# Second routing of a three-layer kernel: flags summed by a full matmul, next thresholds from a base, ScalarE's copies later, and new numbers in the plan that orders the engines

## The chip, the cores and the metric

One core of one Trainium2 chip. The metric is the device time of one execution in microseconds (us). In tables and rows PE is TensorE (PEld its weight loads), DVE VectorE, ACT ScalarE, POOL GpSimd, SP SyncE.

## The reference

An attention with a window and block sums gives 3072 tokens of 512 numbers; a first mixture of 8 experts follows (each token goes to its best expert); the change lies in the second mixture, which gives every expert at most 384 tokens by a greedy order:

```python
def _moe2_ref(x, w_gate, w1, w2):
    N, D = x.shape; E = w_gate.shape[1]; cap = N // E
    logits = x @ w_gate
    flat = logits.flatten(); order = np.argsort(-flat)
    assigned = -np.ones(N, dtype=np.int64); counts = np.zeros(E, dtype=np.int64)
    for idx in order:
        tok, e = (int(idx) // E, int(idx) % E)
        if assigned[tok] >= 0 or counts[e] >= cap: continue
        assigned[tok] = e; counts[e] += 1
        if (assigned >= 0).all(): break
    out = np.zeros((N, D), dtype=np.float32)
    for e in range(E):
        mask = assigned == e
        out[mask] = np.maximum(x[mask] @ w1[e], 0.0) @ w2[e]
    return out
```

## The kernel before

Three stages follow each other: attention (its last matmul with V starts at 166 us of the profile), the first mixture (`phase_b`, to about 310 us), the second mixture (`phase_d`, from 310 us to the end).

**Routing.** The greedy order is found in eight phases (`Route2.phase`, 0 to 7); each fixes one expert and its 384 tokens. A phase takes for every token the best expert still open (`v`, `p_cand`, `p_oh`: tokens lie on 128 partitions x 24 columns). It then seeks a threshold at which some expert is full, in five steps (`NSTEP`). A step lays 31 thresholds on a grid (`p_thr`, L800), compares all tokens with them (`p_g`, L805, 128x768), counts per expert with matmuls (L814 in phase 0, 24 of them; L818 after that, 12 in phases 1 and 2, 6 in phases 3 to 6, where `wide` is 4), takes the counts from what is left in each expert (`p_d`, L821, `p_sat`, L827), and makes of it 31 flags, one for each partition. The number of flags that are set gives the next, finer grid (`th`, L838). In phases 0 and 1 a matmul with ones sums the flags over the partitions (L837). In phases 2 to 6 VectorE does it alone: four copies of the flags (`p_an`, L831), a 32x32 transpose (L832) and a sum (L833). Phase 7 has no search.

After the search `gl` (L843) marks the tokens above the two last thresholds, ScalarE copies it to `p_gl` (L844), `p_og` and `p_rs` (L846, L849) count them, and matmuls sum over partitions (L855) and give positions (L870, L871). ScalarE also turns the one-hot `p_oh` round into `p_ohe` (L794). `Route2.list` makes of the positions the indices of the phase's tokens: matmul into `dx_ps` (L907 or L910), then `p_ix`.

**Expert.** GpSimd gathers the 384 rows in three indirect DMAs (`xg`, L951), TensorE transposes each block of 128 (L962), ScalarE and VectorE split the block in a high and a low part (`dxh`, `dxl`, L965). L1 is 8 groups of 12 matmuls (three for each of 4 slices: L973, L974, L975; 384 columns); after each group ScalarE writes `dhh` (L978) and VectorE `dhl` (L980). L2 is 3 blocks of 24 matmuls (L987 to L989; 512 columns), each with a copy `dz` (L992) and a scatter by GpSimd (L994). Weights are split in high (`wh`, ScalarE, L935) and low (`wl`, GpSimd, L944) parts.

**Order.** Nothing moves at run time: Python code in `phase_d` writes every engine's instructions in one order, by a planned clock. `now` is TensorE's planned time, which each `yield` of `L1` and `L2` moves by a number (0.5 for three L1 matmuls, 0.65 for three L2 matmuls). `dve` and `pool` are the planned ends of VectorE's and GpSimd's work, moved by `busy(x)`. The routing is a thread whose yields give a latency and the TensorE time of what follows; its next part is written when `now` has passed `dve` plus a margin:

```python
        busy(lat); th[1]=dve[0]+(0.4 if curp>0 else 0.1); ...
        if th[0] is not None and now[0]>=th[1]:
            now[0]+=th[3]
```

So the routing of phase p+1 is strewn into the matmuls of expert p or p-1, the gather of an expert comes after its list, and its transposes (`xts_step`) at 4.5 planned us or more behind the gather. Phase 0 and its list have no expert beside them.

## Time and profile before

| | us |
|---|---|
| median of 3 runs | 673.27 |
| lowest, highest | 668.29, 679.38 |
| profiled execution, own time | 666.27 |
| its span | 664.6 |
| TensorE busy in the span | 596.7 |
| VectorE busy | 468.8 |
| GpSimd busy | 384.9 |
| ScalarE busy | 325.0 |

The span is the part of the execution that the profile shows; 1.7 us lie around it. Matmuls overlap in the profile (each lasts longer than the distance to the next), so the distance between starts is what a matmul takes of TensorE. In rows of the time line a bracket at the end gives how long the engine stood idle before the instruction and what released it.

### The profile page before, as it was taken

To read this page: it belongs to the slowest core of one execution; us is meant where nothing else is said; L and a number is where in the kernel's file an instruction comes from. 1 tells how busy PE (TensorE), PEld (TensorE's weight loads), DVE (VectorE), ACT (ScalarE), POOL (GpSimd) and SP (SyncE) were. 2 spreads that over 40 slices of the span, in tenths; PEclk is the share of its full clock that TensorE was granted. 3 is DMA by queue.
4 is the path that set the end of the run, shared out by engine and by line. 5 is a ranking of instruction groups with operands and counts; after the bars stand their busy time and mean duration, and the time that the engine had idled before them with its cause. 6 is when DMAs were issued, how large, how long until landed. Compare 5 with 4: busy or idle time off the path is not lost.

```text
span 664.6 us, 12771 instructions
## 1 busy us (share of the span) xinstructions
PE 596.7 (90%) x4424; PEld 486.6 (73%) x4427; DVE 468.8 (71%) x1811; ACT 325.0 (49%) x704; POOL 384.9 (58%) x424
## 2 busy tenths in 40 slices
PE   7786998999889999997369999999999999999995
PEld 5664877887667777774248788787878878788894
DVE  6774898998796899674766778787878877842110
ACT  5564776888436776640034153542535344263510
POOL 5225654653154688961038196693948759398931
PEclk9788998999789999997579999999999999999998
DMA  9899999939309867700071463515546262476101
GB/s 255 259 231 249 244 286 259 281 94 337 124 16 361 285 245 250 267 20 9 1 247 57 142 207 109 176 65 185 165 143 191 86 192 88 162 253 243 41 0 47
DMA packets 48481, 114.22 MB, mean 172 GB/s; under 512 B 7041, under 2 KB 7809, under 8 KB 48416
## 3 DMA queue, kind: packets, MB, share of 16 engines
q1 hardware_dynamic: 35168, 72.84, 35.5%
...
q14 instruction: 30, 0.25, 0.1%
...
## 4 chain that ended last, share of the span: by engine, by line
PE 23%; DVE 12%; issue 7%; POOL 5%; ACT 3%; DMA 2%; POOLq 0%; DVEq 0%; ACTq 0%
PE dz_ps L987 4%; PE dz_ps L988 4%; PE dz_ps L989 4%; POOL wl L944 4%; PE dh_ps L973 3%; PE dh_ps L975 3%; PE dh_ps L974 3%; ACT wh L935 2%; DVE p_g L805 1%; DVE dhl L980 1%; DVE p_an L831 1%; DMA wraw<-in_w1b_dram 1%; DVE p_d L821 1%; ACT dhh L978 1%; PE rt_ps L818 1%
## 5 line engine op out<-in xcount | busy, mean ns | idle before, releaser
L944 POOL TENSOR_TENSOR wl<-wraw,wh 128x512 fp32r<-128x512 f32 x124 | 155.7, 1294 | 5.4 <-ACT wh L935 5.1
L973 PE MATMUL dh_ps<-dxh,wh 128*128 128x384 f32 x256 | 89.9, 351 | 0.7 <-DVE dxl L965 0.7
L975 PE MATMUL dh_ps<-dxh,wl 128*128 128x384 f32 x256 | 87.5, 342 | 1.3 <-POOL wl L944 1.3
L974 PE MATMUL dh_ps<-dxl,wh 128*128 128x384 f32 x256 | 87.3, 341 | 0.9 <-DVE dxl L965 0.9
L987 PE MATMUL dz_ps<-wh,dhh 128*128 128x512 f32 x192 | 79.6, 415 | 0.0
L989 PE MATMUL dz_ps<-wh,dhl 128*128 128x512 f32 x192 | 75.9, 395 | 0.0
L988 PE MATMUL dz_ps<-wl,dhh 128*128 128x512 f32 x192 | 75.9, 395 | 0.0
L935 ACT CAST wh<-wraw 128x512 fp32r<-128x512 f32 x128 | 74.1, 620 | 3.1 <-DMA wraw<-in_w1b_dram 2.6
L994 POOL DMA_INDIRECT out_dram<-dz,io x24 | 24.4, 1016 | 79.0 <-ACT dz L992 62.5
L980 DVE SCALAR_TENSOR_TENSOR dhl<-dh_ps,dhh 128x384 fp32r<-128x384 f32 x64 | 35.1, 554 | 49.5 <-ACT dhh L978 49.4
L120 POOL TENSOR_TENSOR wraw<-wraw 96x512 f32<-96x512 f32 (+4 forms) x39 | 39.9, 1023 | 51.0 <-DMA wraw<-in_v_dram 48.6
L978 ACT ACTIVATE dhh<-dh_ps 128x384 fp32r<-128x384 f32 x64 | 31.1, 493 | 65.0 <-PE dh_ps L975 65.0
L140 ACT ACTIVATE p_e<-s_sb,nm 128x118 f32<-128x118 f32 x192 | 59.7, 386 | 0.0
L510 POOL TENSOR_TENSOR wl<-wraw,wh 128x1024 fp32r<-128x1024 f32 (+1 forms) x18 | 38.1, 2141 | 27.7 <-ACT wh L509 27.7
L509 ACT CAST wh<-wraw 128x1024 fp32r<-128x1024 f32 (+1 forms) x56 | 49.0, 934 | 7.2 <-DMA wraw<-in_w1a_dram 5.5
L951 POOL DMA_INDIRECT xg<-xrows,p_ix x24 | 23.3, 973 | 48.8 <-DVE rrow L886 29.8
L975 PEld LDWEIGHTS dh_ps<-dxh,wl 128*128 128x128 f32 x256 | 48.7, 190 | 2.7 <-POOL wl L944 2.5
L974 PEld LDWEIGHTS dh_ps<-dxl,wh 128*128 128x128 f32 x256 | 48.7, 190 | 1.7 <-DVE dxl L965 1.4
L973 PEld LDWEIGHTS dh_ps<-dxh,wh 128*128 128x128 f32 x256 | 48.6, 190 | 1.5 <-ACT dxh L965 0.9
L510 DVE TENSOR_TENSOR wl<-wraw,wh 128x1024 fp32r<-128x1024 f32 (+1 forms) x38 | 42.7, 1160 | 6.5 <-ACT wh L509 6.5
L156 PE MATMUL o_ps<-VV,pt_sb 118*64 118x65 f32 x768 | 36.9, 238 | 10.8 <-issue 6.2
L134 DVE CUSTOM_DVE_ANT_0 s_sb<-s_ps,cst 128x118 f32<-128x118 f32 x192 | 42.0, 274 | 4.2 <-PE s_ps L130 2.8
...
## 6 DMA issues: line engine op xcount, KB each, us to landing
...
```

The source lines that it names most:

```text
L134: V.tensor_tensor_reduce(out=sb[:,j,:],in0=p[:,j,0:118],in1=mk,scale=-0.125,scalar=3e38,op0=OP.add,op1=OP.min,accum_out=nm[:,j:j+1])
L140: A.activation(pe[:,j,:],sb[:,j,:],AF.Exp,bias=nm[:,j:j+1],scale=-1.0)
L509: (hi.tensor_copy if hi else nc.scalar.copy)(h[:,c],t[:,c])
L510: (lo or nc.vector).tensor_tensor(l[:,c],t[:,c],h[:,c].bitcast(F32),op=OP.subtract)
L935: A.copy(h[:,c],t[:,c])
L944: eng.tensor_tensor(l[:,c],t[:,c],h[:,c].bitcast(F32),op=OP.subtract)
L973: T.matmul(q,wh[:,c],s['xh'][:,d,:],start=(d==0),stop=False)
L974: T.matmul(q,wh[:,c],s['xl'][:,d,:],start=False,stop=False)
L975: T.matmul(q,wl[:,c],s['xh'][:,d,:],start=False,stop=(d==3))
L987: T.matmul(q,s['hh'][:,f,c0],wh[:,c],start=(f==0),stop=False)
L988: T.matmul(q,s['hh'][:,f,c0],wl[:,c],start=False,stop=False)
L989: T.matmul(q,s['hl'][:,f,c0],wh[:,c],start=False,stop=(f==7))
```

## The change

Five things are changed, all in the second mixture.

- In phases 2 to 6 the flags are summed by the matmul with ones, as in phases 0 and 1; the four copies, the transpose and the sum go. The flags `p_any` are two fixed tiles of 128 rows, cleared once by GpSimd, and the matmul takes all 128 rows.
- A `base` of 33 numbers (next grid laid on the first column of this one) is made while TensorE counts; when the sum comes, one instruction makes the next grid of it (`p_thr`), where two stood in a row (`th`, then `p_thr`). The two last thresholds come from one instruction too.
- ScalarE's `p_ohe` is written at the second step of the search, and `p_gl` after the wait for `p_og`.
- The matmul L855 is written before the four updates of `asg` instead of behind them; `fo` and the update of `rrow` come after the position matmuls.
- The plan's numbers: 0.5 becomes 0.522 for three L1 matmuls, 0.65 becomes 0.7 for three L2 matmuls, the margin 0.4 becomes 0.25, and the latencies of the routing's parts are others.

```diff
@@ Route2.__init__ and init
+        self.anys=[cp.tile([128,1],BF,name=f"p_any{i}") for i in range(2)]
+        for a in self.anys: nc.gpsimd.memset(a,0.0)
...
-        V.tensor_scalar(self.ws,self.wsc,a,2.0,op0=OP.mult,op1=OP.mult)
+        V.tensor_scalar(self.ws,self.wsc,a,2.0,op0=OP.mult,op1=OP.mult); V.tensor_scalar(self.q['ws'],self.wsc,a,2.0,op0=OP.mult,op1=OP.mult)
@@ Route2.phase
-        oh=wk.tile([128,8,24],BF,name="p_ohe"); nc.scalar.copy(oh,oc.rearrange("p c e->p e c"))
+        oh=wk.tile([128,8,24],BF,name="p_ohe")
+        def turn(): nc.scalar.copy(oh,oc.rearrange("p c e->p e c"))
...
-                if s or not ph: V.tensor_scalar(thr,Q('jr'),ws[:,s:s+1],low,op0=OP.mult,op1=OP.add)
...
-                yield ((2.3+0.2*nw if ph>=2 else 1.4) if s else 1.1),(0.7 if ph<1 else 0.8/self.wide(ph))
+                if s==1: turn()
+                yield (1.4 if s else 1.0),(0.1+0.8/n if ph else 0.7)
...
+                if s+1<NSTEP: base=wk.tile([128,33],F32,name="p_base"); V.tensor_scalar(base,Q('jr'),ws[:,s+1:s+2],thr[:,0:1],op0=OP.mult,op1=OP.add)
...
-                if ph>=2:
-
-                    an=wk.tile([128,1],F32,name="p_an4")
-                    for q in range(4): V.tensor_scalar(an[32*q:32*q+R],e,0.0,None,op0=OP.is_ge)
-                    tr=wk.tile([128,32],F32,name="p_tr"); V.transpose(tr,an.to_broadcast([128,32]))
-                    p=wk.tile([128,1],F32,name="p_cnt"); V.tensor_reduce(p,tr[:,0:J],AX.X,OP.add)
-                else:
-                    if ph: V.tensor_scalar(anys,e[0:J],0.0,None,op0=OP.is_ge)
-                    yield (0.7 if ph else 0.35),0.05
-                    p=self.psum(); T.matmul(p[:,0:1],st['ones_b'][0:J,:],anys,start=True,stop=True)
-                V.tensor_scalar(lo,p[:,0:1],ws[:,s:s+1],low,op0=OP.mult,op1=OP.add); low=lo
-            V.tensor_scalar(hi,lo,ws[:,NSTEP-1:NSTEP],None,op0=OP.add)
+                    V.tensor_scalar(anys[0:J],e,0.0,None,op0=OP.is_ge)
+                yield (0.27+0.2*n if ph else 0.35),(0.13 if ph else 0.05)
+                p=self.psum(); T.matmul(p[:,0:1],st['ones_b'],anys,start=True,stop=True)
+                if s+1<NSTEP:
+                    thr=wk.tile([128,33],F32,name="p_thr"); V.scalar_tensor_tensor(thr,Q('ws')[:,s:s+1].to_broadcast([128,33]),p[:,0:1],base,op0=OP.mult,op1=OP.add)
+                else: V.scalar_tensor_tensor(th,Q('ws')[:,s:s+1].to_broadcast([128,2]),p[:,0:1],thr[:,0:2],op0=OP.mult,op1=OP.add)
...
-        nc.scalar.copy(gs,gl)
...
-        if ph: yield (2.5 if 2<=ph<7 else 1.3 if ph else 1.0),0
+        if ph: yield 1.1,0
+        nc.scalar.copy(gs,gl)
...
-        yield 1.0,0.05
-        p=self.psum(); T.matmul(p[:,0:16],st['ones_b'],rs.rearrange("p s e->p (s e)"),start=True,stop=True)
...
-        V.tensor_sub(self.r,self.r,p[:,8:16])
-        yield 1.0,0.1
+        yield 2.1,0.15
         o=p[:,16:18]
         T.matmul(o,st['tri_b'],t2,start=True,stop=False,skip_group_check=True)
@@ phase_d, L1 and step
-            if d<3: yield 0.5
+            if d<3: yield 0.522
...
-        busy(lat); th[1]=dve[0]+(0.4 if curp>0 else 0.1); th.append(dur) if len(th)==3 else th.__setitem__(3,dur)
+        busy(lat); th[1]=dve[0]+(0.25 if curp>0 else 0.1); th.append(dur) if len(th)==3 else th.__setitem__(3,dur)
```

What that does to the order is seen at three places. The first is VectorE in phase 3, from the flags of the fourth step to the differences of the fifth. Before:

```order
L827 ISA p_e 32x1
L831 TENSOR_SCALAR p_an_6230<-p_e 32x1 x4
L832 STREAM_TRANSPOSE p_tr<-p_an_6230 128x32
L833 TENSOR_REDUCE p_cnt<-p_tr 128x1
L838 TENSOR_SCALAR th<-p_cnt,ws,th 128x1
L800 TENSOR_SCALAR p_thr<-st_ps,ws,th 128x32
L805 TENSOR_TENSOR p_g<-st_ps,p_thr 128x768
L980 SCALAR_TENSOR_TENSOR dhl<-dh_ps,dhh 128x384 x2
L821 TENSOR_TENSOR p_d<-rrow,rt_ps 32x8
```

And now (L824 is the line of `p_d`, L826 of `p_sat`, L974 of `dhl`):

```order
L826 ISA p_e 31x1
L827 TENSOR_SCALAR p_any_4617<-p_e 31x1
L974 SCALAR_TENSOR_TENSOR dhl<-dh_ps,dhh 128x384
L831 SCALAR_TENSOR_TENSOR p_thr<-st_ps,rt_ps,p_base 128x33
L806 TENSOR_TENSOR p_g<-st_ps,p_thr 128x768
L974 SCALAR_TENSOR_TENSOR dhl<-dh_ps,dhh 128x384
L824 TENSOR_TENSOR p_d<-rrow,rt_ps 32x8
```

Eight instructions between flags and comparison (with the four copies) have become one, and a `dhl` now stands ahead of `p_thr`, where both stood behind `p_g`.

The second place is TensorE at the first two transposes of phase 4's list. Before (L818 counts, L962 transposes):

```order
L818 MATMUL rt_ps<-p_oh,p_g 128x32
L987 MATMUL dz_ps<-wh,dhh 128x512
L988 MATMUL dz_ps<-wl,dhh 128x512
L989 MATMUL dz_ps<-wh,dhl 128x512
L962 MATMUL dh_ps<-cb,xg 128x128 x4
L987 MATMUL dz_ps<-wh,dhh 128x512
L988 MATMUL dz_ps<-wl,dhh 128x512
L989 MATMUL dz_ps<-wh,dhl 128x512
L962 MATMUL dh_ps<-cb,xg 128x128 x4
```

Now (L829 sums the flags, L956 transposes):

```order
L981 MATMUL dz_ps<-wh,dhh 128x512
L982 MATMUL dz_ps<-wl,dhh 128x512
L983 MATMUL dz_ps<-wh,dhl 128x512
L829 LDWEIGHTS ones_b
L829 MATMUL rt_ps<-p_any_4616,ones_b 128x1
L956 MATMUL dh_ps<-cb,xg 128x128 x4
L981 MATMUL dz_ps<-wh,dhh 128x512
L982 MATMUL dz_ps<-wl,dhh 128x512
L983 MATMUL dz_ps<-wh,dhl 128x512
L956 MATMUL dh_ps<-cb,xg 128x128 x4
```

Between the list's matmuls (L910, now L904) and the first of these transposes there stood 24 L2 matmuls and two counts; now 18 L2 matmuls, one count and one flag matmul.

The third is ScalarE at the start of phase 6. Before (L794 is `p_ohe`, L900 the list's, L992 `dz`):

```order
L978 ACTIVATE dhh<-dh_ps 128x384 x4
L794 COPY p_ohe<-p_oh 128x192
L900 ACTIVATE l_bv<-l_bh,cc 128x24x12
L992 COPY dz<-dz_ps 128x512
L935 CAST wh<-wraw 128x512 x2
```

Now (L796 is `p_ohe`, L894 the list's, L986 `dz`):

```order
L972 ACTIVATE dhh<-dh_ps 128x384 x4
L894 ACTIVATE l_bv<-l_bh,cc 128x24x12
L972 ACTIVATE dhh<-dh_ps 128x384
L796 COPY p_ohe<-p_oh 128x192
L959 CAST dxh<-dh_ps 128x4x128 x2
L986 COPY dz<-dz_ps 128x512
```

`p_ohe` stood ahead of the list's ScalarE step, and stands behind it now.

## Rows read from the trace of the kernel before

**Rows 1.** Busy us (instructions) of PE, PEld, DVE, ACT, POOL; granted clock, DMA share, GB/s.

```profile
588.00:617.00 29.00, 29.00 (x156) 26.70 (x156) 7.87 (x20) 13.55 (x26) 25.48 (x25) 1.00 0.63 228
```

**Rows 2.** TensorE's waits from 312 us on: us in total, times, longest.

```profile
PE rt_ps L855 <- DVE p_rs L849: 6.4, 5, 2.3
...
PE rt_ps L870 <- DVE rrow L867: 3.7, 7, 1.8
...
PE dh_ps L962 <- DMA xg<-xrows,p_ix: 2.6, 3, 0.9
...
PE dh_ps L975 <- POOL wl L944: 1.3, 3, 0.4
```

**Rows 3.** Time line, phase 0: from the sum of flags to the next comparison.

```profile
319.47 0.28 DVE L838 TENSOR_SCALAR th<-rt_ps,ws,th 128x1 f32<-128x1 f32 x1 [0.25 <-PE rt_ps L837]
...
320.13 0.56 DVE L805 TENSOR_TENSOR p_g<-st_ps,p_thr 128x384 bf16<-128x384 f32 x1
```

**Rows 4.** Time line, TensorE: the flags' matmul between L1 matmuls, phase 1.

```profile
362.44 0.34 PE L974 MATMUL dh_ps<-dxl,wh 128*128 128x384 f32 x1
362.61 0.34 PE L975 MATMUL dh_ps<-dxh,wl 128*128 128x384 f32 x1
362.88 0.17 PE L837 MATMUL rt_ps<-p_any,ones_b 31*128 31x1 bf16 x1
...
363.26 0.34 PE L974 MATMUL dh_ps<-dxl,wh 128*128 128x384 f32 x1
```

**Rows 5.** Time line, TensorE: one small matmul between L2 matmuls.

```profile
576.41 0.40 PE L988 MATMUL dz_ps<-wl,dhh 128*128 128x512 f32 x1
576.64 0.40 PE L989 MATMUL dz_ps<-wh,dhl 128*128 128x512 f32 x1
576.88 0.18 PE L855 MATMUL rt_ps<-p_rs,ones_b 128*128 128x16 bf16 x1
...
577.23 0.40 PE L988 MATMUL dz_ps<-wl,dhh 128*128 128x512 f32 x1
```

**Rows 6.** Time line: a list's matmul, gathers, and transposes that use them.

```profile
339.67 0.95 POOL L951 DMA_INDIRECT xg<-xrows,p_ix  x1 [0.30 <-issue]
...
343.54 0.33 PE L962 MATMUL dh_ps<-cb,xg 128*128 128x128 f32 x1 [0.94 <-DMA xg<-xrows,p_ix]
...
575.84 0.34 PE L910 MATMUL dx_ps<-l_bv,l_A 128*128 128x96 bf16 x4
...
578.13 1.01 POOL L951 DMA_INDIRECT xg<-xrows,p_ix  x1 [2.19 <-DVE st_ps L856]
...
580.71 0.95 POOL L951 DMA_INDIRECT xg<-xrows,p_ix  x1 [0.30 <-PE dz_ps L989]
...
582.30 0.27 PE L962 MATMUL dh_ps<-cb,xg 128*128 128x128 f32 x1
...
585.61 0.44 PE L962 MATMUL dh_ps<-cb,xg 128*128 128x128 f32 x2 [0.89 <-DMA xg<-xrows,p_ix]
```

**Rows 7.** Time line, ScalarE and VectorE ahead of a wait for L849.

```profile
481.31 0.20 ACT L844 COPY p_gl<-st_ps 128x48 f32<-128x48 f32 x1 [3.48 <-DVE st_ps L843]
...
482.31 1.14 ACT L935 CAST wh<-wraw 128x512 fp32r<-128x512 f32 x2
...
483.87 0.56 DVE L980 SCALAR_TENSOR_TENSOR dhl<-dh_ps,dhh 128x384 fp32r<-128x384 f32 x1 [0.86 <-ACT dhh L978]
484.35 0.54 DVE L849 TENSOR_REDUCE p_rs<-p_og 128x16 bf16<-128x384 bf16 x1
```

**Rows 8.** Time line: last matmul of an L1 group, its `dhl`; and a step's differences and flags.

```profile
360.52 0.34 PE L975 MATMUL dh_ps<-dxh,wl 128*128 128x384 f32 x1
...
361.42 0.56 DVE L980 SCALAR_TENSOR_TENSOR dhl<-dh_ps,dhh 128x384 fp32r<-128x384 f32 x1 [0.31 <-ACT dhh L978]
...
424.96 0.17 DVE L821 TENSOR_TENSOR p_d<-rrow,rt_ps 32x8 f32<-32x8 f32 x1 [0.94 <-PE rt_ps L818]
...
425.74 0.14 DVE L831 TENSOR_SCALAR p_an<-p_e 32x1 f32<-32x1 f32 x1
```

More of the change, by code (lines that the diff above doesn't have):

```diff
@@ L308, in load_const @@
     wg=cp.tile([128,32],F32,name="wg2"); nc.sync.dma_start(wg,I['wg2']); st['wg2']=wg
-    cc=cp.tile([128,38],F32,name="cc"); nc.sync.dma_start(cc,I['cc']); st['cc']=cc
+    cc=cp.tile([128,6],F32,name="cc"); nc.sync.dma_start(cc,I['cc']); st['cc']=cc
 def make_const(nc,cp,st):
@@ L739, in layout_c @@
 def layout_c(inp):
-    jr=np.tile(np.arange(1,33,dtype=np.float32),(128,1))
     ws=np.tile(np.array([2.0/32**(s+1) for s in range(5)],np.float32),(128,1))
     p0=np.arange(128,dtype=np.float32)[:,None]
-    return dict(cc=np.ascontiguousarray(np.concatenate([jr,ws,p0],1)),w1b=np.ascontiguousarray(inp['moe2_w1']),w2b=np.ascontiguousarray(inp['moe2_w2']))
+    return dict(cc=np.ascontiguousarray(np.concatenate([ws,p0],1)),w1b=np.ascontiguousarray(inp['moe2_w1']),w2b=np.ascontiguousarray(inp['moe2_w2']))
 class Route2:
@@ L793, in phase @@
         oc=wk.tile(B3,BF,name="p_oh"); V.tensor_tensor(oc,cand,mx[:,:,None].to_broadcast(B3),op=OP.is_equal)
-        oh=wk.tile([128,8,24],BF,name="p_ohe"); nc.scalar.copy(oh,oc.rearrange("p c e->p e c"))
+        oh=wk.tile([128,8,24],BF,name="p_ohe")
+        def turn(): nc.scalar.copy(oh,oc.rearrange("p c e->p e c"))
         th=self.th; lo=th[:,0:1]; hi=th[:,1:2]; ws=self.ws
         if ph<7:
-            low=self.nM
+            n=self.wide(ph) if ph else 1; thr=self.thr0
+            if ph==0: V.tensor_scalar(thr,Q('jr'),ws[:,0:1],self.nM,op0=OP.mult,op1=OP.add)
+            yield 1.2,0
             for s in range(NSTEP):
-                thr=wk.tile([128,32],F32,name="p_thr") if s else self.thr0
-                if s or not ph: V.tensor_scalar(thr,Q('jr'),ws[:,s:s+1],low,op0=OP.mult,op1=OP.add)
-                if s==0: yield 1.1,0
                 g=wk.tile([128,24,32],BF,name="p_g")
@@ L804, in phase @@
                     B=[128,c1-c0,32]
-                    V.tensor_tensor(g[:,c0:c1],v[:,c0:c1,None].to_broadcast(B),thr[:,None,:].to_broadcast(B),op=OP.is_ge)
+                    V.tensor_tensor(g[:,c0:c1],v[:,c0:c1,None].to_broadcast(B),thr[:,None,1:33].to_broadcast(B),op=OP.is_ge)
                 if s==0: next(inq,None)
-                nw=self.wide(ph) if ph>=1 else 1
-                yield ((2.3+0.2*nw if ph>=2 else 1.4) if s else 1.1),(0.7 if ph<1 else 0.8/self.wide(ph))
-                p=self.psum()
-                anys=wk.tile([J,1],BF,name="p_any")
-                if ph<1:
-                    if ph==0: T.matmul(p[0:J,0:8],st['mone'][:,0:J],st['capr'],start=True,stop=False)
-                    for c in range(24): T.matmul(p[0:J+(ph>0),0:8],g[:,c,0:J+(ph>0)],oc[:,c,:],start=(ph>0 and c==0),stop=(c==23))
+                if s==1: turn()
+                yield (1.4 if s else 1.0),(0.1+0.8/n if ph else 0.7)
+                p=self.psum(); anys=self.anys[s%2]
+                if ph==0:
+                    T.matmul(p[0:J,0:8],st['mone'][:,0:J],st['capr'],start=True,stop=False)
+                    for c in range(24): T.matmul(p[0:J,0:8],g[:,c,0:J],oc[:,c,:],start=False,stop=(c==23))
                 else:
-                    n=self.wide(ph)
                     for c in range(0,24,n): T.matmul(p[0:32*n,0:8*n],g[:,c:c+n,:].rearrange("p c j->p (c j)"),oc[:,c:c+n,:].rearrange("p c e->p (c e)"),start=(c==0),stop=(c==24-n))
+                if s+1<NSTEP: base=wk.tile([128,33],F32,name="p_base"); V.tensor_scalar(base,Q('jr'),ws[:,s+1:s+2],thr[:,0:1],op0=OP.mult,op1=OP.add)
+                if ph==0:
+                    sat=wk.tile([J,8],BF,name="p_sat")
+                    V.tensor_scalar(sat,p[0:J,0:8],0.0,0.0,op0=OP.is_ge,op1=OP.max,accum_out=anys[0:J])
+                else:
                     d=wk.tile([128,8],F32,name="p_d"); x=self.r
@@ L963, in xT @@
         c=slice(128*b,128*b+128); h=S[p]['xh'][:,:,c]
-        busy(0.65)
+        busy(0.72)
         A.copy(h,q); V.tensor_tensor(S[p]['xl'][:,:,c],q,h.bitcast(F32),op=OP.subtract)
@@ L975, in L1 @@
             T.matmul(q,wl[:,c],s['xh'][:,d,:],start=False,stop=(d==3))
-            if d<3: yield 0.5
+            if d<3: yield 0.522
         h=s['hh'][:,f,:]
         A.activation(h,q,AF.Relu)
-        busy(0.5)
+        busy(0.6)
         V.scalar_tensor_tensor(s['hl'][:,f,:],q,0.0,h.bitcast(F32),op0=OP.max,op1=OP.subtract)
-        yield 0.5
+        yield 0.522
     def L2(p,b):
@@ L1062, in phase_d @@
     while True:
-        if route[0] is None and route[2]<7 and (route[2] in routed if route[2] else 0 in listed): R.update(); busy(1.4); start_route(route[2]+1)
+        if route[0] is None and route[2]<7 and (route[2] in routed if route[2] else 0 in listed): R.update(); busy(1.25); start_route(route[2]+1)
         if (curp>=0 or xts.get(0,3)==3 or now[0]<gath_t[0]+HOLD) and try_thread(): continue
```

26 lines of the change are left out of this document (13 added, 13 removed).

## The prediction

> **What bounds the kernel now.** I read the busy time by stage first. Once routing is over, between 588 and 617 us, TensorE is busy for 29.00 of 29.00 us at a granted clock of 1.00 (2.4 GHz), with VectorE at 7.87 and GpSimd at 25.48 [rows 1]. From the first expert on, TensorE sets the pace, and routing costs time where its matmuls take TensorE's time or keep TensorE waiting. So the list of TensorE's waits comes next. From 312 us on it waits 6.4 us at L855 (five times, the longest, 2.3, in phase 0, where nothing runs beside), 3.7 at L870 (seven times, 1.8 of it in phase 0), 2.6 for gathered rows and 1.3 for `wl` [rows 2]. Beside experts that leaves 4.1 + 1.9 + 1.3 us that a better order could win, and 0.9 for gathers [rows 6]. VectorE, which the change relieves most, is no bound: a shorter chain on it pays only where TensorE now waits for it, and in phase 0.
>
> **Phase 0.** Its chain lies bare. From the sum of flags, `th` starts at 319.47 and the comparison at 320.13, 0.66 us for two instructions, the first of 0.28 [rows 3]. One instruction at half that distance, 0.33, takes their place, in four steps, and the end of the search loses one as well: 5 x 0.33 = **-1.65 us**. The `base` lies between a comparison and its count, where VectorE waits for TensorE; were it not hidden, 4 x 0.33 would be lost again. The second `ws` and L870's freedom from `rrow` are one small instruction each way and cancel.
>
> **The waits that go.** Ahead of L855 I follow one case. ScalarE reaches the copy `p_gl` early and stands 3.48 us idle at it; casts and `dhh` pile up behind, so a `dhl` starts only at 483.87 after 0.86 us of waiting, and `p_rs` behind it at 484.35 [rows 7]. The copy is now written later, when `gl` is done, and L855 stands 15 L1 matmuls behind the last flags. `p_rs` takes 0.54 [rows 7], and th, `gl` and `p_og` ahead of it, with no more elements than `p_rs` reads, no longer each: at most 4 x 0.54 = 2.2 us, and 15 x 0.17 + 0.3 = 2.9 are there; a `dhl` of 0.56 between them about fits. So **-4.1 us**; if a wait stays, 0. L870 loses its wait for `rrow` and stands 15 matmuls behind L855 in place of 9: **-1.9**. `wl` is needed at the start of an expert's L1. Around phase 4's list 48 L2 matmuls now stand between the first transpose and that L1, where 15 stood: 33 x 0.23 = 7.6 us more for GpSimd, **-1.3**.
>
> **The flags' matmul, 25 new ones (5 phases x 5 steps).** Among L1 matmuls: from L975 at 362.61 to L974 at 363.26 are 0.65 us with the flags' matmul in it, where two matmuls take 2 x 0.17 (362.44 to 362.61): 0.30 us [rows 4]. Among L2 matmuls no such one is in the trace; the nearest is a matmul with the same weights and 16 columns, 576.64 to 577.23, 0.59 against 2 x 0.23: 0.13 us [rows 5]. In the new order 9 of the 25 stand among L1, 16 among L2 or transposes: 9 x 0.30 + 16 x 0.13 = **+4.8 us**; ends 25 x 0.13 = 3.3 and 25 x 0.30 = 7.5. The matmul takes 128 rows of flags in place of 31, which L855 has too.
> The Trainium skill, in "TensorE: Matmul & The Clock Gate" (Back-to-back issue gap; LDWEIGHTS), gives a matmul of up to 64 columns an issue floor of some 25 ns, and a load of 128 columns 128/1.2 = 107 ns. An estimate from that page is 0.13 us wherever the matmul stands, 3.3 us in all, 1.5 less than I take; the rows among L1 speak against it.
>
> **Transposes that come too early.** This is the largest cost. In the trace a list's matmul starts at 575.84, the first gather at 578.13 (2.3 us later: VectorE makes the indices), and the first transpose, 6.46 us after the list's matmul, just runs [rows 6]. A gather takes 3.87 us from its start to a transpose that waited for it (339.67 to 343.54), at most 4.17 (578.13 to 582.30, no wait), once 4.90 (580.71 to 585.61) [rows 6]. So the rows are there 2.3 + 3.9 = 6.2 us after the list's matmul. In the new order there are between list and first transpose, for phase 4, 18 L2 matmuls, one count (six small matmuls, which I put at two of the one in [rows 5], 0.26) and one flags' matmul: 0.34 + 18 x 0.23 + 0.26 + 0.13 = 4.9 us. TensorE waits 1.3 us there. The other transposes stand 1.1 to 1.4 us behind, where gathers come every 1.3 (578.13 to 580.71 are two); only in phases 2 and 3 the second and third stand side by side, which adds 0.8. By the same count, with 18 to 21 L2 matmuls ahead of each first transpose (phase 6: 15 and 6 of L1): phase 1 0.4, 2 and 3 1.3 each, 4 and 5 1.4 each, 6 1.3; together 7.1, less the 0.9 that was waited: **+6.2 us**. At 3.4 us for a gather it is some 3, at 4.9 some 12.
>
> **Flags behind a `dhl`.** A step used to wait for VectorE once, at the count; now twice. A `dhl` written right behind its L1 group can't start before ScalarE's `dhh` is done: 0.90 us after the group's last matmul starts (360.52 to 361.42), and lasts 0.56 [rows 8]. The count starts 0.2 after that matmul, so `p_d` behind such a `dhl` starts 1.3 us into it; flags take 0.78 from `p_d` (424.96 to 425.74) and 0.14 + 0.1 [rows 8], 2.3 us in all, and TensorE is there after 0.26 + 9 x 0.17 + 0.1 = 1.9. That is 0.4 us at three places (phases 2, 3, 4), and by the same reckoning 0.2 at two counts behind a `p_thr` that stands behind a `dhl`, and 0.2 in phase 6: **+1.8 us**. With a cast (0.6) ahead of `dhh` each time it is 5. Where a `dhl` is an older one, nothing is waited.
>
> **Rest at nothing.** `p_ohe` is needed only at `p_og`, over a step later. The clearing of the flags' tiles lies on an idle GpSimd. Five fewer VectorE instructions a step, 0.14 to 0.28 each [rows 3, 8], free some 25 x 1 us on an engine that isn't the bound.
>
> **Sum.** -1.65 - 4.1 - 1.9 - 1.3 + 4.8 + 6.2 + 1.8 = **+3.85 us** on the profiled execution of 666.27, 670.1. The median of the runs shown is 673.27, 7.0 above that execution; the same step from there gives **677 us**, 0.6% more than before.
>
> **Rivals.**
> A, the gathers land in time. If a gather takes 3.5 us or the list's indices come sooner, and no `dhl` is in the way, the transposes cost 1 us and the flags 3.3: -8.95 + 4.3 = -4.65, 668.6 us. For it: the waiting gather of 3.87 was in a stage of little traffic, but none shorter waited in these rows. Against: in the trace the order gives a list 6.46 us and leaves nothing over.
> B, the waits are moved, not gone. `p_gl` reads a PSUM tile that VectorE works on as well; VectorE's update L848 has to wait for the copy, which may stand behind ScalarE's casts of 1.14 us [rows 7]. Then the position matmul is late by 1.14 less the 0.55 that its 15 matmuls leave over, six times: +3.5 on the forecast, 680.5 us. The Trainium skill, in "PSUM — Partial Sum Buffer" (PSUM bank collisions raise a hardware error), says that two engines may not be in one bank and quadrant at once, reads included; the diff's order leaves that wait to L848, and no row here shows its length.
> C, slower: gathers take 4.9 us as the one in phase 6 did, since the weights' loads run beside them. Six lists wait 12 us in place of 6.2, with casts ahead of `dhh` 3 more: 3.85 + 9 = +12.8, 686 us. It decides from 5.0 us on: then TensorE loses over 2%.
> D, the change doesn't shorten what paces: that holds beside experts in any case; were the routing chain itself the pace there, the 25 us above would be won, 648 us. Against it: TensorE's waits in [rows 2] are too short for that.
>
> **How the numbers follow.** Forecast (+1 to +7 us: 674 to 680) 0.50, A 0.22, B 0.14, C 0.10, D 0.01, the rest unknown. The range takes A's with the lowest run seen (668.29, 5 below the median) and C's: 665 to 687. A measurement of this kernel tells about 2% from no change, 13.5 us. Faster by more: D and an A with a low run, 0.04; slower by more: half of C and a B with C's gathers, 0.08; within 2% 0.88.
>
> **What would show it.** In the changed profile: waits at L846 and L862 (the old L855, L870) near zero; 35 flags' matmuls, VectorE's busy time down by 20 us or more; waits at L956 for gathered rows in five or six lists, 0.4 to 1.3 us each; waits at L829 of some 0.4. Wrong would make it: gathers landing within 3 us (A), long waits at L862 for L848's chain (B), an L956 that waits 3 us (C), or a routing whose lists come so late that an expert's start waits.

## The result, and the profile after

| | before | after |
|---|---|---|
| median of 20 runs each, us | 671.72 | 675.50 |
| lowest, highest | 667.68, 679.38 | 669.14, 684.84 |
| profiled execution, own time | 666.27 | 672.59 |
| TensorE busy | 596.7 | 601.6 |
| VectorE busy | 468.8 | 445.5 |

The ratio is 1.0054, with a 95% interval of 1.0027 to 1.0080: 3.6 us more (1.8 to 5.4). The two profiled executions lie 6.3 us apart, so their times alone don't measure it. VectorE has 23 us less to do (in a step of phases 2 to 6 its eight instructions between `p_e` and `p_g` have become two, `p_any` and `p_thr`, with `base` beside them), TensorE 4.9 more, and where no routing runs the picture is that of [rows 1]: TensorE 29.00 of 29.00 us.

TensorE's waits from 312 us on, in the changed kernel (us in total, times, longest):

```profile
PE dh_ps L956 <- DMA xg<-xrows,p_ix: 6.3, 7, 1.5
PE rt_ps L829 <- DVE p_any L827: 3.7, 4, 2.7
...
PE rt_ps L846 <- DVE p_rs L843: 3.3, 2, 1.8
PE rt_ps L815 <- DVE p_g L806: 2.2, 6, 0.6
...
PE rt_ps L862 <- DVE p_ei L858: 1.4, 1, 1.4
```

Against [rows 2]: the waits for p_rs have shrunk from 6.4 to 3.3 (1.8 of it is phase 0, 1.5 phase 7, which has no search), those for rrow and wl are gone (1.4 for p_ei is phase 0). In their place stand 6.3 for gathered rows (4.8 beside experts; 0.9 before), waits for the flags (3.7, of which 2.7 in expert 0) and for a comparison (2.2; 0.3 before).

The clearest view is a sum over stretches, since attention and the first mixture, which the change doesn't touch, end at 310 to 320 us, a few us apart from one execution to the next. The table takes the starts of rows in the time lines: from the reduction L734 (end of the first mixture) to expert 0's first L1 matmul, from there to expert 1's, and so on, up to the end of the last L2 matmul (its start and 0.24). Each line is one profiled execution; two of them (before, again, 676.2 us, and flags with 31 rows, 688.0) ran slower than most executions of their kernels.

| us | L734 to expert 0 | expert 0 | experts 1 to 5 | 6 and 7 | ratio, 95% interval |
|---|---|---|---|---|---|
| before | 33.4 | 45.9 | 197.7 | 68.2 | 1 |
| before, again | 34.8 | 45.9 | 198.4 | 68.2 | |
| after | 30.9 | 49.1 | 203.9 | 68.9 | 1.0054 (1.0027 to 1.0080) |
| after, again | 31.0 | 46.5 | 203.7 | 68.9 | 1.0070 (1.0034 to 1.0106) |
| transposes later | 31.8 | 48.4 | 197.6 | 68.9 | 1.0011 (0.9975 to 1.0047) |
| casts behind dhh | 31.0 | 48.3 | 203.7 | 68.9 | 1.0067 (1.0033 to 1.0101) |
| copies only | 32.6 | 47.9 | 192.6 | 68.3 | 0.9891 (0.9843 to 0.9939) |
| old plan | 31.7 | 46.6 | 218.4 | 71.4 | 1.0351 (1.0300 to 1.0402) |
| copies and base | 31.8 | 46.2 | 191.5 | 68.9 | 0.9919 (0.9880 to 0.9957) |
| same, idle flags' matmuls | 31.9 | 48.1 | 191.7 | 69.6 | 0.9919 (0.9883 to 0.9954) |
| later, flags on VectorE | 31.0 | 53.4 | 197.4 | 68.9 | 1.0018 (0.9979 to 1.0056) |
| flags with 31 rows | 31.6 | 51.2 | 207.9 | 68.9 | 1.0124 (1.0085 to 1.0163) |
| copies, base, order of sums | 31.4 | 46.7 | 194.3 | 68.9 | 0.9878 (0.9819 to 0.9937) |
| copies and base, same place | 31.3 | 49.2 | 191.6 | 68.3 | 0.9874 (0.9810 to 0.9937) |

Experts 1 to 5 repeat within 0.7 us for one order, so they tell orders apart where the times can't; expert 0 doesn't repeat (46.5 and 49.1 for the same kernel). From before to after: 2.4 to 3.9 us won in the first column, 0.6 to 3.2 lost in expert 0, 5.3 to 6.1 in experts 1 to 5, 0.6 in 6 and 7. Not all of this is the change's own. In the first column the first matmul of phase 0 starts 0.7 us after L734 in some executions and 1.4 to 1.5 in others, with either order; both profiles of before have the long one and both of after the short one, and before, again has a gather that landed late. With the same start the change wins 1.6 us there (33.4 before, 31.8 in the run with transposes later). And one count of phase 2, 12 matmuls and 0.7 us, has moved from expert 0 to expert 1.

Four places of the changed kernel's time line show where. Phase 0, VectorE, from the sum of flags to the next comparison; it answers to [rows 3], and 0.66 us from start to start have become 0.29:

```profile
317.74 0.26 DVE L831 SCALAR_TENSOR_TENSOR p_thr<-st_ps,rt_ps,p_base 128x33 f32<-128x33 f32 x1 [0.26 <-PE rt_ps L829]
318.03 1.09 DVE L806 TENSOR_TENSOR p_g<-st_ps,p_thr 128x384 bf16<-128x384 f32 x3
```

The flags' matmul among L1 matmuls (for [rows 4]) and among L2 matmuls. From L969 at 402.50 to L968 at 402.97 are 0.47 us for two L1 matmuls of 0.175, so the flags cost 0.12; from L983 at 460.12 to L982 at 460.72 0.60 for two of 0.23, so 0.14:

```profile
402.50 0.33 PE L969 MATMUL dh_ps<-dxh,wl 128*128 128x384 f32 x1
402.67 0.18 PE L829 MATMUL rt_ps<-p_any,ones_b 128*128 128x1 bf16 x1
402.71 0.42 PE L967 MATMUL dh_ps<-dxh,wh 128*128 128x384 f32 x1
402.97 0.34 PE L968 MATMUL dh_ps<-dxl,wh 128*128 128x384 f32 x1
...
460.12 0.40 PE L983 MATMUL dz_ps<-wh,dhl 128*128 128x512 f32 x1
460.36 0.18 PE L829 MATMUL rt_ps<-p_any,ones_b 128*128 128x1 bf16 x1
460.40 0.48 PE L981 MATMUL dz_ps<-wh,dhh 128*128 128x512 f32 x1
460.72 0.40 PE L982 MATMUL dz_ps<-wl,dhh 128*128 128x512 f32 x1
```

A list's matmul, its gathers and the first transpose, phase 6 (for [rows 6]). The gather starts 4.3 us after the list's matmul here (VectorE makes the first masks of phase 7 ahead of the indices), the rows are used 4.0 after that, and TensorE has stood 1.52 us at the transpose:

```profile
570.58 0.43 PE L904 MATMUL dx_ps<-l_bv,l_A 128*128 128x96 bf16 x6
...
574.91 1.00 POOL L945 DMA_INDIRECT xg<-xrows,p_ix  x1 [5.92 <-DVE p_ix L911]
...
578.95 0.66 PE L956 MATMUL dh_ps<-cb,xg 128*128 128x128 f32 x4 [1.52 <-DMA xg<-xrows,p_ix]
```

And expert 0, which the prediction left out. ScalarE stands 3.41 us at the casts of the second half of w1, whose load lands at 344.5; the first `dhh` comes behind them, `dhl` behind that, `p_d` and the flags behind `dhl`, and TensorE stops for 2.69 us:

```profile
344.50 2.18 ACT L929 CAST wh<-wraw 128x512 fp32r<-128x512 f32 x4 [3.41 <-DMA wraw<-in_w1b_dram]
...
346.59 0.48 ACT L972 ACTIVATE dhh<-dh_ps 128x384 fp32r<-128x384 f32 x1
347.10 0.56 DVE L974 SCALAR_TENSOR_TENSOR dhl<-dh_ps,dhh 128x384 fp32r<-128x384 f32 x1 [4.42 <-ACT dhh L972]
347.91 0.15 DVE L824 TENSOR_TENSOR p_d<-rrow,rt_ps 32x8 f32<-32x8 f32 x1
...
348.49 0.18 PE L829 MATMUL rt_ps<-p_any,ones_b 128*128 128x1 bf16 x1 [2.69 <-DVE p_any L827]
```

Then TensorE is granted the lower clock. By windows (columns as in rows 1), 0.50 is 1.2 GHz, and TensorE was busy for 0.26 and 1.06 of 2 us ahead of it:

```profile
345.55:347.55 2.00, 0.26 (x2) 0.00 (x0) 0.45 (x1) 1.94 (x5) 2.00 (x2) 1.00 1.02 381
347.55:349.55 2.00, 1.06 (x7) 1.06 (x8) 1.59 (x8) 0.62 (x1) 2.00 (x3) 1.00 0.39 145
349.55:351.55 2.00, 2.00 (x18) 1.54 (x16) 1.19 (x3) 1.52 (x3) 2.00 (x3) 0.54 0.03 12
351.55:353.55 2.00, 2.00 (x6) 1.70 (x6) 0.46 (x4) 0.00 (x0) 2.00 (x2) 0.50 0.00 0
```

### The profile page after: what moved, and what is told of

It is laid out like the page before. It is cut to its first block, busy times and chain, and to the rows that moved or that the text cites. A ratio compares the mean times of both kernels' runs of the same rounds, so it can differ in the third digit from the quotient of the medians.

```text
span 670.8 us, 12694 instructions
## 1 busy us (share of the span) xinstructions
PE 601.6 (90%) x4452; PEld 488.1 (73%) x4452; DVE 445.5 (66%) x1680; ACT 326.4 (49%) x704; POOL 387.5 (58%) x428
## 4 chain that ended last, share of the span: by engine, by line
PE 20%; issue 11%; POOL 11%; DVE 5%; DMA 3%; ACT 2%; POOLq 0%; DVEq 0%; ACTq 0%
POOL wl L938 9%; PE dh_ps L967 3%; PE dh_ps L968 3%; PE dh_ps L969 3%; PE dz_ps L981 3%; PE dz_ps L982 3%; PE dz_ps L983 3%; DMA xg<-xrows,p_ix 2%; ACT wh L929 1%; PE dh_ps L956 1%; DMA wraw<-in_w1b_dram 1%; POOL out_dram L988 1%; DVE p_g L806 1%; PE rt_ps L813 0%; PE rt_ps L815 0%
## 5 line engine op out<-in xcount | busy, mean ns | idle before, releaser
L968 PE MATMUL dh_ps<-dxl,wh 128*128 128x384 f32 x256 | 87.8, 343 | 1.2 <-DVE dxl L959 1.2
L969 PE MATMUL dh_ps<-dxh,wl 128*128 128x384 f32 x256 | 87.5, 342 | 0.0
L974 DVE SCALAR_TENSOR_TENSOR dhl<-dh_ps,dhh 128x384 fp32r<-128x384 f32 x64 | 35.6, 556 | 67.4 <-ACT dhh L972 66.7
L983 PE MATMUL dz_ps<-wh,dhl 128*128 128x512 f32 x192 | 76.0, 396 | 0.0
L982 PE MATMUL dz_ps<-wl,dhh 128*128 128x512 f32 x192 | 75.9, 395 | 0.0
L929 ACT CAST wh<-wraw 128x512 fp32r<-128x512 f32 x128 | 72.4, 619 | 7.1 <-DMA wraw<-in_w1b_dram 6.1
L972 ACT ACTIVATE dhh<-dh_ps 128x384 fp32r<-128x384 f32 x64 | 31.4, 491 | 74.7 <-PE dh_ps L969 66.1
L968 PEld LDWEIGHTS dh_ps<-dxl,wh 128*128 128x128 f32 x256 | 49.0, 191 | 2.0 <-DVE dxl L959 1.7
L986 ACT COPY dz<-dz_ps 128x512 f32<-128x512 f32 x24 | 14.1, 586 | 71.7 <-PE dz_ps L983 34.1
L969 PEld LDWEIGHTS dh_ps<-dxh,wl 128*128 128x128 f32 x256 | 48.9, 191 | 0.0
```

The source lines that it names most:

```text
L929: A.copy(h[:,c],t[:,c])
L968: T.matmul(q,wh[:,c],s['xl'][:,d,:],start=False,stop=False)
L969: T.matmul(q,wl[:,c],s['xh'][:,d,:],start=False,stop=(d==3))
L982: T.matmul(q,s['hh'][:,f,c0],wl[:,c],start=False,stop=False)
L983: T.matmul(q,s['hl'][:,f,c0],wh[:,c],start=False,stop=(f==7))
```

## The experiments

**Transposes later.** In the changed kernel, experts 1 to 7:

```diff
-        if ... now[0]>=gath_t[q]+4.5+1.0*xts[q] ...
+        if ... now[0]>=gath_t[q]+(6.2 if q else 4.5)+1.0*xts[q] ...
```

> The changed kernel with one number altered: the transposes of experts 1 to 7 are written 6.2 planned us behind their gather in place of 4.5. Theory (transposes stand too early): in the profile of the changed kernel TensorE waits 6.3 us for gathered rows, some 4.85 of them beside experts; with five to nine more L2 matmuls between list and transposes these go to under 1 us, a gain of about 4 us, from 1.005 to about 0.999 of the kernel before. Rival (the rows are late for a reason of their own, and whatever is written behind them waits): the wait stays or goes to the L1 that needs the transposed rows, and the ratio stays at 1.005.

The waits for gathered rows fell from 6.3 to 1.8 us, none of it beside experts, and experts 1 to 5 from 203.9 to 197.6. Part of these 6.3 us has only moved into expert 0: the count of phase 2 (0.7) and the wait ahead of expert 1's L1 shown below. Experts 0 to 5 together take 246.0 us, where the second profile of the changed kernel has 250.2: 4.2 less, as the theory says. The ratio, 1.001, agrees, but its interval (0.9975 to 1.0047) overlaps the changed kernel's. One expert shows that later isn't free. In phase 1 the transposes now stand right ahead of expert 1's L1, which waits 2.22 us for the high part of the rows and then runs for 3.4 us at 1.2 GHz, 0.32 us a matmul:

```profile
397.30 0.66 PE L956 MATMUL dh_ps<-cb,xg 128*128 128x128 f32 x4
400.18 0.44 PE L967 MATMUL dh_ps<-dxh,wh 128*128 128x384 f32 x1 [2.22 <-ACT dxh L959]
400.90 0.69 PE L968 MATMUL dh_ps<-dxl,wh 128*128 128x384 f32 x1 [0.28 <-DVE dxl L959]
401.39 0.52 PE L969 MATMUL dh_ps<-dxh,wl 128*128 128x384 f32 x1
401.71 0.52 PE L967 MATMUL dh_ps<-dxh,wh 128*128 128x384 f32 x1
```

**Casts behind dhh.** In the changed kernel:

```diff
-        if q==0: return g+4.3+2.9*j if j else f+4.3
+        if q==0: return g+8.0+2.9*j if j else f+4.3
...
-            if npc==32 and conved[curp]<12 or ...
+            if npc==16 and conved[curp]<8 or npc==32 and conved[curp]<12 or ...
...
-            if xts.get(q,0)==3 and conved.get(q,0)>=8:
+            if xts.get(q,0)==3 and conved.get(q,0)>=(8 if q else 4):
```

> The changed kernel, but expert 0 may start when the first chunk of its w1 is split, and the second chunk's casts are planned 8.0 + 2.9 us behind the gather (they were planned at 4.3 + 2.9; the chunk lands 10.9 us behind it). Theory: the four casts that wait 3.4 us for the load no longer stand ahead of ScalarE's first dhh, so the flags' matmul at 348.49 loses its wait of 2.69 us, and TensorE, which doesn't stop, keeps its 2.4 GHz between 349 and 356, where it now starts L1 matmuls 0.32 us apart in place of 0.175 (some 3 us lost): together a gain of 4 to 6 us, a ratio of 0.996 to 1.000. Rival 1 (the clock falls there whatever is waited for): only the 2.7 us, 1.001. Rival 2 (the second chunk's low half is late and the fifth L1 group waits for it): no gain, 1.005.

Nothing was won: 1.0067, expert 0 takes 48.3 us. The flags' wait is gone. But TensorE's clock fell all the same, 1.0 us into L1 and for 3.4 us, with no wait for flags near it, and at the end of expert 0 eight of expert 1's transposes now stand side by side ahead of a count of phase 2, which waits 1.84 us for its comparison:

```profile
390.37 1.42 PE L956 MATMUL dh_ps<-cb,xg 128*128 128x128 f32 x8
393.63 0.55 PE L815 MATMUL rt_ps<-p_oh,p_g 128*64 128x16 bf16 x12 [1.84 <-DVE p_g L806]
```

Rival 1 is right that the clock falls anyway, but neither rival says the rest: the loss moved to another wait of the same expert.

**Copies only.** The kernel before, with

```diff
-        oh=...; nc.scalar.copy(oh,oc.rearrange("p c e->p e c"))
+        def turn(): nc.scalar.copy(oh,oc.rearrange("p c e->p e c"))
...
+                if s==1: turn()
...
-        nc.scalar.copy(gs,gl)
...
         if ph: yield (2.5 if 2<=ph<7 else 1.3 if ph else 1.0),0
+        nc.scalar.copy(gs,gl)
```

> The kernel before with ScalarE's two copies placed as in the change (p_ohe at the second step, p_gl behind the wait for p_og) and nothing else. Theory (the copies are what delayed p_rs): the 4.1 us of waits at the matmul on p_rs beside experts go, 667.6 us where before takes 671.7, a ratio of 0.994; a trace shows that wait at under 1 us beside phase 0's 2.3. Rival (p_rs was late because its chain on VectorE is long, and the copies only lay beside it): the waits stay, ratio 1.000.

Better than the theory by time, 0.9891, or 7.3 us. The profile shows 5 us less of waits for p_rs and rrow beside experts 1 to 5, and 4.0 to 6.0 us less from L734 to the end (341.3 against 345.3 and 347.3); where the rest of the 7.3 lies is open. TensorE's order is that of before, and of the waits for p_rs (L858 here) only phase 0's is left; each wait for rrow beside experts 1 to 5 has halved as well (0.34 to 0.17). The run moves both copies, and both stood waiting in the kernel before (ScalarE idle for 37 us in all ahead of `p_ohe`, 32 ahead of `p_gl`); what each is worth alone it doesn't tell. Its waits from 312 us on:

```profile
PE rt_ps L873 <- DVE rrow L870: 2.8, 7, 1.8
...
PE rt_ps L858 <- DVE p_rs L852: 2.1, 1, 2.1
```

**Old plan.** The changed kernel with 0.5, 0.65 and 0.4 for 0.522, 0.7 and 0.25.

> The changed kernel with the plan's old numbers for TensorE and the margin (0.5, 0.65, 0.4 in place of 0.522, 0.7, 0.25); all else stays. In this order 21 L2 matmuls, two counts and a flags' matmul stand between a list and its first transposes (18 to 21, one and one in the changed kernel), but two transposes stand side by side five times. Theory (what costs is how the transposes stand, not the numbers as such): the waits for gathers stay at 4 to 5 us, the flags' waits shrink by 1 us: ratio 1.003 to 1.005. Rival (the new time model itself is the loss): ratio 0.998 or below.

Both theories fail, and in the other direction than the rival said: 1.035, 23 us slower than before. With the old numbers the same planned time covers more matmuls, and the latencies of the routing's parts, which stay new here, were set for the others. The lists of phases 2 to 6 stand behind 48 to 51 of an expert's 72 L2 matmuls, in the changed kernel behind 24, 15, 6, none and none; so the transposes end up against the next L1, and that costs twice, in waits and in clock:

```profile
477.38 0.66 PE L956 MATMUL dh_ps<-cb,xg 128*128 128x128 f32 x4 [1.49 <-DMA xg<-xrows,p_ix]
...
478.09 1.12 PE L956 MATMUL dh_ps<-cb,xg 128*128 128x128 f32 x4
479.88 0.69 PE L967 MATMUL dh_ps<-dxh,wh 128*128 128x384 f32 x1 [0.67 <-ACT dxh L959]
481.92 0.69 PE L968 MATMUL dh_ps<-dxl,wh 128*128 128x384 f32 x1 [1.35 <-DVE dxl L959]
482.40 0.52 PE L969 MATMUL dh_ps<-dxh,wl 128*128 128x384 f32 x1
```

Experts 2 to 5 in its windows (the last three numbers are clock, DMA share, GB/s), at 0.93 to 0.99 where the changed kernel has 1.00:

```profile
436.46:479.88 43.42, 39.80 (x224) 32.27 (x224) 25.91 (x98) 18.55 (x37) 28.16 (x29) 0.98 0.41 138
479.88:523.93 44.05, 40.27 (x224) 33.46 (x225) 28.45 (x102) 14.54 (x30) 27.90 (x28) 0.94 0.37 127
523.93:567.40 43.47, 39.30 (x224) 32.04 (x224) 25.88 (x98) 18.47 (x37) 28.04 (x29) 0.99 0.41 140
567.40:612.73 45.33, 40.60 (x214) 33.34 (x214) 27.98 (x109) 16.78 (x34) 28.68 (x29) 0.93 0.39 132
```

**Copies and base.** The changed kernel with the flags of phases 2 to 6 on VectorE, the plan's old numbers and latencies, and the sums where they were:

```diff
-                    V.tensor_scalar(anys[0:J],e,0.0,None,op0=OP.is_ge)
+                if ph>=2:
+                    an=wk.tile([128,1],F32,name="p_an4")
+                    for q in range(4): V.tensor_scalar(an[32*q:32*q+32],e,0.0,None,op0=OP.is_ge)
+                    tr=wk.tile([128,32],F32,name="p_tr"); V.transpose(tr,an.to_broadcast([128,32]))
+                    p=wk.tile([128,1],F32,name="p_cnt"); V.tensor_reduce(p,tr[:,0:J],AX.X,OP.add)
```

> The kernel with only ScalarE's copies moved, and to it the base and the one-instruction threshold of the change, the flags summed on VectorE as before; TensorE's order is that of the kernel before to the row. Theory (the base pays in phase 0, where nothing runs beside, and nowhere else): phase 0 shorter by 1.65 to 2.5 us, some 661 us, a ratio of 0.985 to 0.987. Rival (a shorter chain pays beside experts as well, since flags and lists come sooner): more than 4 us below the run with the copies alone, 0.983 or less; a second rival, no gain because expert 0's weights land no sooner: 0.989.

0.9919, not to be told from the copies alone by time, and outside the theory's range. The trace shows what the base pays: a step of phase 0's search takes 2.18 us (the flags' matmuls start at 322.91 and 325.09) where before takes 2.54, and experts 1 to 5 gain 1.0 us at most. So the theory's place is right, and the gain too small to be seen in the times.

**Idle flags' matmuls.** To the last kernel, ahead of the counts of phases 2 to 6:

```diff
+                    if ph>=2: T.matmul(p[:,300:301],st['ones_b'],anys,start=True,stop=True)
```

> As the run with copies and base, and 25 idle flags' matmuls beside it: in phases 2 to 6 a matmul of the ones with a flags' tile that nobody reads stands ahead of each step's counts (it adds work that the result doesn't need). Nothing waits for them and no order changes, so they show the price of the matmul alone. Theory (a fixed 0.13 us each): 3.3 us more than without, a ratio higher by 0.005. Rival 1 (0.30 us, as the row in phase 1 before): 7.5 us, higher by 0.011. Rival 2 (beside the counts they are nearly free, 0.04 us): 1 us, higher by 0.0015.

The second rival is right. Among L1 and L2 matmuls alike the counts of phases 3 to 6 with an idle matmul take 0.28 us, without it 0.25: 0.03 each, and experts 1 to 5 agree as a sum (191.7 against 191.5; single ones differ by up to 1.5, where a gather or a wait for `wl` fell otherwise). So of the 0.13 us that a lone flags' matmul costs, some 0.10 is the break in the row of L1 or L2 matmuls. One of the idle matmuls and its counts:

```profile
511.44 0.18 PE L815 MATMUL rt_ps<-p_any,ones_b 128*128 128x1 bf16 x1
511.47 0.30 PE L816 MATMUL rt_ps<-p_oh,p_g 128*128 128x32 bf16 x6
```

**Flags on VectorE in the new order.** Transposes later as in the first run, and the flags' diff of the run with copies and base.

> The changed kernel with the transposes written later (as in the first run) and with the flags of phases 2 to 6 summed on VectorE as before (its latencies in the plan as before). Theory (what is left of the loss is the flags' matmuls, 3.3 us, and the waits for flags and for counts behind a dhl, 3): some 5 us below the run with late transposes alone, a ratio of 0.992 to 0.995. Rival (the shorter chain is what lets the lists come in time, so VectorE's flags bring other waits): 1.000 or above.

By time the rival: 1.0018, and experts 1 to 5 at 197.4 against 197.6. The 25 matmuls and, beside experts 1 to 5, the waits for flags are gone; waits for p_rs have grown, 5.7 us in six against 4.5 in four. But the clock differs: expert 1 runs for 10.2 us at 1.2 GHz here, and for 3.4 in the run with late transposes, and takes 43.3 us against 41.7; experts 2 to 5, at a clock of 1.00 in both, take 154.1 against 155.9. So where the clock is the same the flags on VectorE win 1.8 us, and what the clock took in expert 1 (and in expert 0, 53.4 us at a clock of 0.87) hides it. Whether that loss belongs to the order is open; the medians, 672.85 and 673.20, show no gain. The 6.1 us of experts 1 to 5 that lie between transposes later and copies and base (197.6, 191.5) are then, as an estimate from the rows, 23 flags' matmuls of 0.13 (3.0), the lower clock in expert 1 (1.7) and 1.8 more of waits, 0.4 too much in sum.

**The changed kernel again.** No edit.

> The changed kernel once more, for a second profile of the same order. Theory (the wait of 2.69 us for expert 0's first flags is not the change's: the load's landing against the start of L1 differs from one execution to the next): this profile shows another wait there, between 0 and 2.7 us, while the waits for gathered rows beside experts stay at 4 to 5 us; the ratio lies between 1.003 and 1.008. Rival (that wait belongs to the order): 2.5 us or more again.

The theory's numbers: 1.40 us in place of 2.69, and experts 1 to 5 repeat to 0.3 us each. Its reason is not borne out: the other runs that move the copies wait there too, 0.55 to 2.85 us, but for the one with the casts behind. What sets the length is said at the second profile of the kernel before, below.

**Flags with 31 rows.** In the changed kernel:

```diff
-                p=self.psum(); T.matmul(p[:,0:1],st['ones_b'],anys,start=True,stop=True)
+                p=self.psum(); T.matmul(p[:,0:1],st['ones_b'][0:J],anys[0:J],start=True,stop=True)
```

> The changed kernel, but the flags' matmul takes 31 rows of ones and flags in place of 128, as the one of the kernel before did in phase 1. TensorE's order is that of the changed kernel. The row in phase 1 of the kernel before showed 0.30 us among L1 matmuls; the changed kernel shows 0.13 at most of its flags' matmuls, among L1 and L2 alike. Theory (the 31 rows are what made it 0.30): some 0.17 us more at each of 30 flags' matmuls beside experts, 5 us, a ratio higher than the changed kernel's by 0.007 (1.012 to 1.015); the trace shows 0.30 in place of 0.13. Rival (a load's time goes by its columns, not by its rows; the 0.30 was a short wait for the flags): 0.13 as before, the ratio unchanged at 1.005 to 1.007.

The theory: 1.0124, and each flags' matmul that stands alone costs 0.30 us where it cost 0.13. Experts 1 to 5 take 4.1 us more than in the changed kernel, but that this is near 23 x 0.17 = 3.9, for the 23 that lie in them, is partly luck: expert 1 ran for 3.4 us at 1.2 GHz in this profile, which by itself makes it some 1.7 longer (half of 3.4), and the waits came out 0.8 shorter. The same place as in phase 2 above, a flags' matmul between L1 matmuls; from L969 at 415.65 to L968 at 416.31 are 0.66 us, so 0.31:

```profile
415.65 0.34 PE L969 MATMUL dh_ps<-dxh,wl 128*128 128x384 f32 x1
415.92 0.09 PEld L829 LDWEIGHTS <-ones_b 31*128 31x128 bf16 x1 [0.25 <-issue]
415.92 0.17 PE L829 MATMUL rt_ps<-p_any,ones_b 31*128 31x1 bf16 x1
416.02 0.44 PE L967 MATMUL dh_ps<-dxh,wh 128*128 128x384 f32 x1
416.31 0.34 PE L968 MATMUL dh_ps<-dxl,wh 128*128 128x384 f32 x1
```

**Copies, base and the order of the sums.** The run with copies and base, with L846 ahead of the updates and `fo` and `rrow` behind the position matmuls.

> The run with copies and base, and to it the order of the change on VectorE around the sums: the matmul on p_rs ahead of the four updates, fo and the update of rrow behind the position matmuls. TensorE's order is still that of the kernel before. Theory (the wait for rrow ahead of the position matmuls is the update's, and goes with it): 0.16 us of wait and 0.15 of delay less at each of six position matmuls, 1.5 to 2 us, some 0.002 below the run with copies and base; the trace shows no wait for rrow. Rival (the updates now stand between p_rs and p_ei, so the position matmul waits for p_ei): waits of the same size there, no gain.

The rival, and more than it said: the wait for rrow is gone, and one of 0.54 to 0.57 for p_ei stands in its place (0.17 for rrow in the run without), in expert 5 two, of 0.91 and 0.46. Experts 1 to 5 take 2.8 us more, and these waits are 2.7 of it. The ratios of the two runs, 0.9878 and 0.9919, can't show it. In the changed kernel the position matmul doesn't wait beside experts because its latency in the plan, 2.1, puts it 15 matmuls behind L846 and not 9.

**The kernel before again.** No edit.

> The kernel before once more, for a second profile. Theory (expert 0's first wait and TensorE's clock in it differ from one execution to the next, the rest is set by the order): a wait of 0 to 2.7 us for the first flags, and the same waits as in the first profile from expert 1 on: 4 of about 1 us for p_rs, six of 0.16 to 0.35 for rrow; from the end of the first mixture to the last L2 matmul 343 to 348 us, where the first profile has 345.3 and the changed kernel has 352.7 and 350.0. Rival (the order alone sets it): 345.3 within 0.5.

The theory for all but expert 0: from expert 1 on the waits repeat to 0.1 us but for one gather that landed 0.7 later, and the stretch is 347.3 us. Expert 0 has no wait for flags again, and 45.84 us after 45.93. That doesn't show the old order free of it. In both profiles of before the lower clock begins 0.8 to 0.9 us into L1, so TensorE reaches the first flags only 6.2 us after L1's start, and they are just ready then (6.1 and 6.3). In the other runs they are ready after 6.3 to 7.7 us. Where the lower clock comes ahead of them there, TensorE arrives after 6.1 to 6.9 us and waits 0 to 1.5; where it comes only later, TensorE arrives after 4.6 to 4.7 and waits 2.3 to 2.9. So how long it waits goes with where the clock falls, and the flags come up to 1.5 us later in the new orders; what the order before would wait at 2.4 GHz no run shows.

**Same place.** To the run with copies and base:

```diff
+        pad=wk.tile([128,224],F32,name="pad"); nc.gpsimd.memset(pad[0:1,0:1],0.0)
```

> The run with copies and base again, with an unused tile of 896 bytes a partition ahead of the second mixture's work tiles. In every kernel made from the changed source, experts 6 and 7, beside which no routing runs, take 35.04 and 33.82 us, in the kernel before and in the one with the copies alone 34.80 and 33.45; L1 matmuls of expert 7 start 176.6 ns apart against 173.5, at a granted clock of 1.00 in both. The new constants moved dxh, dxl, dhh and dhl by 128 bytes; the unused tile moves them to where they lay before, up to a multiple of 1024. Theory (the place of these tiles sets the pace): 34.80 and 33.45 again, some 0.25 to 0.35 us less in each of eight experts, 2 to 3 us in all, a ratio lower by 0.003 to 0.005 than the 0.992 of the run without the tile. Rival (the pace has another cause): 35.04 and 33.82.

Experts 6 and 7 take 34.81 and 33.44 us again: the theory. Beside routing little comes of it (191.6 after 191.5, 0.4 more of gathers' waits in it), so 1 us in all and not 2 to 3. The unused tile moves all work tiles behind it, so which of them counts is not told. Within the intervals the ratio of 0.9874 is that of the run without the tile. This kernel, the copies alone and the run with copies and base all beat both kernels, the one before by about 1%.

## Why the prediction was right, and where its terms were not

The time (677 forecast, 675.5 measured; +3.85 us forecast, +3.6 by the runs) and the course of it were right: waits at p_rs and rrow go, transposes written too early and flags behind a `dhl` bring as much and more. Several terms were mis-sized, others were left out, and that they cancel to 0.3 us is luck.

- **Phase 0, -1.65.** Measured -1.6 at expert 0's first L1 matmul. From the first flags' matmul to the one on p_rs 10.8 us in place of 12.6 (the shorter wait for p_rs is in it); the first step is 0.3 longer, ahead of the position matmul 0.3 is won. Right, and the two small terms cancel as said.
- **The waits that go, -4.1, -1.9, -1.3.** The copies alone take the 4.1 at p_rs away, as forecast; in the changed kernel 1.5 came back in phase 7, whose p_rs now stands behind phase 6's indices on VectorE. The waits at L870 (now L862) and at `wl` are gone beside experts.
- **The flags' matmul, +4.8.** Mis-sized: 0.12 to 0.14 us nearly everywhere, 25 x 0.13 = 3.3, the lower end. The five of phase 1 fell from 0.30 to 0.13 with the change as well, up to 5 x 0.17 = 0.85 us that the prediction didn't count (two show it; the others stand at a wait or at the lower clock). The step that failed is the price among L1 matmuls: the 0.30 of [rows 4] belongs to a matmul of 31 rows, and the prediction, which saw that the new one takes 128 rows like L855, gave it the price of the 31 rows among L1 matmuls all the same. The estimate of 3.3 us from the Trainium skill, "TensorE: Matmul & The Clock Gate" (Back-to-back issue gap; LDWEIGHTS), was the better one.
- **Transposes too early, +6.2.** Right in kind, too large in size: waits of 4.8 us beside experts in both profiles against 0.9, +4.0, and the 60 transposes of experts 1 to 5 take 1.2 us more themselves (6.6 from start to start, waits left out, in place of 5.4). List by list it is less right: 0, 1.3, 0.4, 0.9, 0.7 and 1.5 us for phases 1 to 6, where 0.4, 1.3, 1.3, 1.4, 1.4 and 1.3 were forecast. In phases 4 and 5 the gathers took 3.3 to 3.5 us and not 3.9; in phase 6 the size agrees by luck, since its gather starts 4.3 us behind the list's matmul and not 2.3. The run with later transposes took the waits beside experts away.
- **Flags behind a dhl, +1.8.** Too small: from expert 1 on 1.0 us at the flags and 2.2 at comparisons, +3.2. The prediction counted the flags' waits and took two of the others at 0.2; there are six, 0.15 to 0.6.
- **Left out.** Expert 0 (+0.6 to +3.2): ScalarE's casts of the load's second half begin 3.4 to 3.5 us into its L1, where they began 1.4 and 2.5 us into it before, and the first flags are ready 7.3 to 7.4 us into it in place of 6.1 to 6.3; why, beyond the load's landing, no run tells. And 0.6 us in experts 6 and 7 from the place of the work tiles.
- **The plan's numbers** were priced only through the places at which instructions stand. That was enough for the forecast, but not for knowing what they are worth: with the old ones beside the new latencies 20 us are lost, with the old latencies too, and the flags on VectorE (copies and base), none.

Rival A, with gathers in time, is the run with later transposes, +0.7 us and not -4.65. The prediction weighed it with a wrong reading: the waiting gather of 3.87 us was not in a stage of little traffic (DMA share 0.76 and 212 GB/s from 339 to 344 us, 0.50 and 153 from 575 to 586), and the same trace holds one of 3.56 us (338.38 to 341.94) that TensorE waited 0.80 for. B didn't come: L862 doesn't wait beside experts. C's 4.9 us didn't come either: the gathers at which TensorE waited beside experts took 3.3 to 4.6. D is refuted: with VectorE's longer chain back, in the run of the new order, experts 1 to 5 took as long.
